# Moving float32 splits and a weight conversion between VectorE, GpSimd and two stages of a fused attention and two-MoE kernel

## The chip, the cores and the metric

The kernel runs on one core of one Trainium2 chip. The metric is the device time of one execution in microseconds (us). Of the core's engines these appear: TensorE (PE in the profile, with PEld for the loads of its weights), VectorE (DVE), ScalarE (ACT), GpSimd (POOL) and SyncE (SP), which issues most of the DMAs.

## What is computed

Three layers follow each other. An attention between `x` (4 batches, 8 heads, 512 positions, 64 lanes) and 32 state rows per batch gives 2176 tokens of 512 numbers. A dense mixture of 8 experts, whose weights P come from a softmax that is balanced eight times over rows and columns, follows, and then one wide gated layer:

```python
# first MoE
for e in range(E):                       # 8 experts, d_ff 1024
    h = np.maximum(x @ w1[e], 0.0)
    out += P[:, e:e + 1] * (h @ w2[e])
# second MoE: w_in 512x2048 and w_out 2048x512 are float64
h = x @ w_in
g = h * (1.0 / (1.0 + np.exp(-h)))
return g @ w_out
```

Products are made to float32 accuracy from three passes. Each operand is split into a high part (`fp32r`, a rounding) and a low part (the operand less its high part), and low times high, high times low and high times high are added up. So every operand costs a cast on ScalarE and a subtraction on another engine. The subtractions are what the change moves.

## The kernel before

The experts are cut into 16 units `u` of 512 hidden columns (two per expert), each with four 128x512 blocks of `w1` and four of `w2`. The work goes through five stages, of which four matter.

**Start and units 0 and 1 (0 to 250 us).** Attention, the first products, and units 0 and 1 for all four batches.

**Units 2 to 15 for batches 0 and 1 (some 252 to 840 us).** One unit takes some 47 us and has eight steps `k`: two batches times four blocks `f`. Step by step the loop at lines 1125 to 1263 issues: `S1` two steps ahead (the hidden block `ph`, its cast `hh` on ScalarE at L705, its low part `hl` on VectorE at L706), then `S2` (12 matmuls into four banks `po`). After the fourth block the four banks are weighted and added into `acc` by four VectorE instructions at L745. The pool `ps2` has four banks, so the next batch's first `S2`, and the state rows' product at k = 3, wait for these additions. At a unit's end k goes from 7 to 0 of the next unit. Weights are loaded ahead (`load_w1`, `load_w2`): the cast of a block is L243 on ScalarE, its low part is `lo_of` at L96, on the engine that `load_split` is given. In the kernel before this is VectorE for unit 1's `w1` and for `w2` of units 0 and 1, and GpSimd for all others. GpSimd also makes sums of `w2` blocks and their low parts (L213, L220) and the low parts of `G` (L668 through L96).

**The conversion.** `w_in` and `w_out` arrive as float64. A generator, `convert_all`, turns them into float32 high and low parts by integer operations on VectorE (L302 to L307: six instructions on 128x512 for one block, then L330 and L334, or L319 and L320, and for each pair of blocks the sums at L351 to L360) and stores them to DRAM. It has 40 items, ten for each quarter `v` of the hidden columns, and yields twice per item. In the kernel before `convert_some` draws it forward at 86 places: eight in unit 1 and six in each of units 2 to 14, with a pace of 0.99 yields per place, and `convert_some` puts each instruction behind the last `hl` on VectorE and the last `hh` on ScalarE.

**Batches 2 and 3 (some 840 to 1320 us).** A seven-product scheme (`block`, `product_b`) for the same units. The change doesn't touch it.

**Second MoE (some 1320 us to the end).** 16 phases `q`, of which the first eight are for the first half of the tokens; the phases 0 and 1 use the converted quarter v = 0, 2 and 3 use v = 1, and 6 and 7 use v = 3. A phase has seven products of six matmuls in the order 1, 5, 2, 6, 3, 7, 4 with the four parts of `second` (12 matmuls each, of the phase before) between them. `silu` makes a gated block: a sigmoid (L819), a product on VectorE (L820), a cast `gh` on ScalarE (L823) and the low part `gl` on VectorE (L824 through L96). The four banks of `ps2` hold the results `pr`, which VectorE adds into `res` (L851). In the first eight phases the state rows' product `s_second` comes right after the last part of `second` and takes a bank of the same pool.

TensorE's order is written out by hand. On the other engines a planner orders the instructions by the place where they are written and by its own estimate of when each becomes ready; the order is fixed before the kernel runs.

Of the kernel before, what the change touches and what calls it, by code (L numbers as in the profile page):

```python
# [21 lines left out]
def fused_kernel(ctx: ExitStack, tc: tile.TileContext, x, state, w_gate, w1, w2, w_in, w_out, out):  # L22
# [240 lines left out]
    def load_w1(u, hp, only_raw=False):  # L263
        e, fh = divmod(u, UPE)
        src = w1[e, hp * 128:(hp + 1) * 128, fh * FU:(fh + 1) * FU]
        if only_raw:
            load_raw(src, [128, FU], f"w1_{u}_{hp}")
        else:
            w1t[u, hp] = load_split(src, [128, FU], f"w1_{u}_{hp}", "w1", 4, nc.vector if u == 1 else nc.gpsimd)

    def load_w2(u, f, only_raw=False):
        e, fh = divmod(u, UPE)
        r0 = fh * FU + f * 128
        if only_raw:
            load_raw(w2[e, r0:r0 + 128, :], [128, DM], f"w2_{u}_{f}")
        else:
            w2t[u, f] = load_split(w2[e, r0:r0 + 128, :], [128, DM], f"w2_{u}_{f}", "w2", 5, nc.vector if u < UPE else nc.gpsimd)

# [102 lines left out]

    def ask_next(n):
        for one in items[n + 1:n + 3]:
            if one[0] is not item_sums:
                ask(one[1])
                return

    def convert_all():

        before = None  # L390
        for n in range(len(items) + 1):
            now, ops = None, []
            if n < len(items):
                make, *args = items[n]
                now = make(*args)
                ops = next(now)
            half = (len(ops) + 1) // 2
            if before:
                next(before)
            for op in ops[:half]:  # L400
                op()
            opens = n < len(items) and (items[n][0] is item_in and items[n][-1] == 0 or n and items[n - 1][0] is item_sums)
            if not opens:
                ask_next(n)
            yield
            for op in ops[half:]:
                op()
            if before:
                stored.append(next(before))
            if opens:  # L410
                ask_next(n)
            yield
            before = now
# [365 lines left out]
    def product(q, p):  # L779
# [23 lines left out]
        elif p == 5:  # L803
            kept("s5", "att", att)
        elif p == 2:
# [3 lines left out]
        elif p == 3:  # L809
            silu(q, 0, 1, summed("c12", ps, parts["u2"]))  # L810
        elif p == 7:
            kept("u3", "att", att)
            silu(q, 1, 1, summed("c22", parts["u3"], parts["s5"]))
        else:
            silu(q, 1, 0, ps)

    def silu(q, f, c, src):
        sg = att.tile([128, 512], F32, tag="e2", name=f"sg{q}_{f}_{c}", bufs=3)
        nc.scalar.activation(out=sg, in_=src, func=AF.Sigmoid)  # L819
        nc.vector.tensor_tensor(out=sg, in0=src, in1=sg, op=ALU.mult)  # L820
        hh = hp_.tile([128, 512], F32R, tag="hh", name=f"gh{q}_{f}_{c}")
        hl = hp_.tile([128, 512], F32R, tag="hl", name=f"gl{q}_{f}_{c}")
        nc.scalar.copy(hh, sg)  # L823
        lo_of(hl, sg, hh)  # L824
        blocks[q, f, c] = hh, hl
# [258 lines left out]

    convert_ops = convert_all()
    pace = 1.04 * 2 * (len(items) + 1) / (8 + (NU - UPE - 1) * 6)
    done = [0, 0]

    def convert_some():
        with tc.issue_after(last["dve"].ins), behind_rows():  # L1090
# [237 lines left out]
    s_load(0, 1)  # L1328

    for q, (g, v, fp) in enumerate(phases):  # L1330
        more = q + 1 < len(phases)
        earlier = [lambda: None] * 4 if q == 0 else [lambda n=n: second(q - 1, n) for n in range(4)]

        def step(p):
            product(q, p)
            if more:
                load_win(*phases[q + 1][1:], p)
            if q == 7 and p != 4:
                later = {1: 6, 5: 3, 2: 7, 6: 4}.get(p)
# [81 lines left out]
```

## Time and profile before

| | us |
|---|---|
| median of 3 runs | 1684.21 |
| lowest and highest | 1681.69, 1689.62 |
| the profiled execution | 1687.53 |
| its span, first to last instruction | 1685.5 |

| engine | busy us | share of the span | instructions |
|---|---|---|---|
| PE | 1628.7 | 97% | 7269 |
| DVE | 1148.2 | 68% | 1616 |
| ACT | 724.7 | 43% | 1231 |
| POOL | 717.9 | 43% | 455 |

The 97% is an average over stages. In some of them TensorE never stops, and in others it stops for a few microseconds per unit and then runs for a while at the lower clock. So the stages are to be read one by one: how long each engine is busy in it, which clock was granted, what ended TensorE's waits, and what the engine that it waited for did before. An idle GpSimd or ScalarE alone says nothing, and a busy VectorE costs something only where an instruction that TensorE needs stands behind others in its queue.

### The profile page before, as it was taken

The page shows a single profiled execution, that of the slowest core. Times are in us where ns is not written, and L with a number is a line of the kernel's source. Part 1 is how long each engine was busy: PE and PEld are TensorE (multiplying, and loading weights), DVE is VectorE, ACT ScalarE, POOL GpSimd, SP SyncE. Part 2 cuts the span into 40 slices and gives each one's busy share as a digit, 9 for nine tenths or more (in the row PEclk, how much of TensorE's full clock was granted, in tenths as well). Part 3 has the DMA queues.
Part 4 walks back from the last instruction along what each step waited for, and adds up shares of the span by engine and source line. Part 5 has one row for each costly group of instructions (what it writes and reads, how often), then busy time and mean ns, then how long its engine had stood idle before and what let it go on. Part 6 is the DMA issues. An engine that isn't in the chain of part 4 may idle for free.

```text
span 1685.5 us, 20967 instructions
## 1 busy us (share of the span) xinstructions
PE 1628.7 (97%) x7269; PEld 1302.0 (77%) x7269; DVE 1148.2 (68%) x1616; ACT 724.7 (43%) x1231; POOL 717.9 (43%) x455
## 2 busy tenths in 40 slices
PE   7999999899998999989999999999999999999999
PEld 5788777677776777767888888888888788888887
DVE  8924785776777767667636777767767656585565
ACT  5644346344443443434334444444544533343332
POOL 2011256666565655566546767666753400000000
PEclk9999999999999999999999999999999999999999
DMA  7042359757765776766436664544541654445442
GB/s 181 26 141 85 132 180 317 252 203 239 248 227 189 256 256 216 251 215 215 151 107 175 171 172 148 172 148 157 158 144 51 230 174 152 156 150 169 138 142 71
DMA packets 196394, 293.49 MB, mean 174 GB/s; under 512 B 35584, under 2 KB 82240, under 8 KB 196288
## 3 DMA queue, kind: packets, MB, share of 16 engines
q1 hardware_dynamic: 169552, 242.71, 46.0%
q10 hardware_dynamic: 26736, 49.44, 8.0%
q8 instruction: 58, 0.95, 0.2%
q14 instruction: 48, 0.39, 0.1%
HBM read 194.27 MB, written 97.81 MB: 173 GB/s over the span
## 4 chain that ended last, share of the span: by engine, by line
PE 78%; DVE 11%; DMA 3%; issue 3%; ACT 2%; POOL 2%; SPq 0%; ACTq 0%; DVEq 0%; POOLq 0%
PE pBa L980 8%; PE po L91 7%; PE po L92 6%; PE po L93 6%; PE pa L790 5%; PE pBc L980 4%; PE pr L92 3%; PE pr L93 3%; PE pr L91 3%; PE ph L91 3%; PE pB L93 3%; PE pB L91 3%; PE pB L92 3%; PE ph L93 3%; PE ph L92 3%; PE pc L790 3%
## 5 line engine op out<-in xcount | busy, mean ns | idle before, releaser
L91 PE MATMUL po<-h_w,hl 128*128 128x512 f32 x576 | 236.2, 410 | 22.2 <-DVE acc L745 20.7
L92 PE MATMUL po<-l_w,hh 128*128 128x512 f32 x576 | 231.2, 401 | 0.0
L93 PE MATMUL po<-h_w,hh 128*128 128x512 f32 x576 | 230.8, 401 | 0.0
L706 DVE SCALAR_TENSOR_TENSOR hl<-ph,hh 128x512 fp32r<-128x512 f32 x144 | 98.8, 686 | 184.8 <-ACT hh L705 184.6
L705 ACT ACTIVATE hh<-ph 128x512 fp32r<-128x512 f32 x144 | 86.2, 599 | 292.9 <-PE ph L93 289.7
L96 POOL TENSOR_TENSOR l_w<-raw,h_w 128x512 fp32r<-128x512 f32 x104 | 151.0, 1465 | 125.1 <-ACT h_w L243 112.7
L91 PEld LDWEIGHTS po<-h_w,hl 128*128 128x128 f32 x576 | 111.0, 193 | 62.4 <-DVE acc L745 25.7
L96 POOL TENSOR_TENSOR T<-t,T 128x512 fp32r<-128x512 f32 x84 | 113.3, 1349 | 82.1 <-ACT T L943 81.0
L980 PE MATMUL pBa<-T,wh 128*128 128x512 f32 x448 | 139.5, 392 | 0.5 <-DVE T L96 0.5
L93 PEld LDWEIGHTS po<-h_w,hh 128*128 128x128 f32 x576 | 111.4, 193 | 25.2
L92 PEld LDWEIGHTS po<-l_w,hh 128*128 128x128 f32 x576 | 111.6, 194 | 23.3 <-issue 0.2
L91 PE MATMUL ph<-aTh,G 128*128 128x512 f32 x288 | 118.4, 411 | 6.0 <-ACT stg L630 3.1
L943 ACT CAST T<-t 128x512 fp32r<-128x512 f32 x112 | 69.5, 621 | 115.6 <-DVE t L948 101.1
L220 POOL TENSOR_TENSOR w2s<-w2s,w2h 128x512 fp32r<-128x512 f32 x56 | 79.6, 1421 | 89.8 <-ACT w2h L219 86.9
L93 PE MATMUL ph<-aTh,G 128*128 128x512 f32 x288 | 114.0, 396 | 0.0
L92 PE MATMUL ph<-aTl,G 128*128 128x512 f32 x288 | 113.8, 395 | 0.0
L745 DVE SCALAR_TENSOR_TENSOR acc<-po,P,acc 128x512 f32<-128x512 f32 x112 | 77.6, 741 | 39.6 <-PE po L93 39.6
L96 POOL TENSOR_TENSOR G<-gf,G 128x1024 fp32r<-128x1024 f32 x32 | 77.6, 2424 | 60.9 <-ACT G L667 60.9
L93 PE MATMUL pr<-woh,gh 128*128 128x512 f32 x256 | 100.2, 391 | 0.0
L92 PE MATMUL pr<-wol,gh 128*128 128x512 f32 x256 | 100.1, 391 | 0.0
L91 PE MATMUL pr<-woh,gl 128*128 128x512 f32 x256 | 99.9, 390 | 0.0
L980 PEld LDWEIGHTS pBa<-T,wh 128*128 128x128 f32 x448 | 84.1, 188 | 19.8 <-DVE T L96 1.2
(268 smaller groups left out, 3916.9 us busy)
## 6 DMA issues: line engine op xcount, KB each, us to landing
g_d<-stg ACTq DMA_DIRECT2D x60, 512.0 KB, 4.3
wi<-wi_d SPq DMA_DIRECT2D x108, 256.0 KB, 3.0
raw<-in_moe_w_dram SPq DMA_DIRECT2D x104, 256.0 KB, 4.6
gf<-g_d SPq DMA_DIRECT2D x128, 128.0 KB, 4.1
w_d<-w2h ACTq DMA_DIRECT2D x56, 256.0 KB, 2.8
w_d<-w2s SPq DMA_DIRECT2D x56, 256.0 KB, 2.3
gfs<-g_d SPq DMA_DIRECT2D x112, 128.0 KB, 4.1
wh<-w_d SPq DMA_DIRECT2D x56, 256.0 KB, 3.4
```

The costliest lines, as they stand in the source:

```text
L91: nc.tensor.matmul(ps, al, bh, start=first, stop=False)
L92: nc.tensor.matmul(ps, ah, bl, start=False, stop=False)
L93: nc.tensor.matmul(ps, ah, bh, start=False, stop=last)
L96: engine.tensor_tensor(out=lo, in0=src, in1=hi.bitcast(F32), op=ALU.subtract)
L220: nc.gpsimd.tensor_tensor(out=t.bitcast(F32R), in0=t, in1=hi.bitcast(F32), op=ALU.subtract)
L705: last["act"] = nc.scalar.activation(out=hh, in_=ph, func=AF.Relu)
L706: last["dve"] = nc.vector.scalar_tensor_tensor(out=hl, in0=ph, scalar=0.0, in1=hh.bitcast(F32), op0=ALU.max, op1=ALU.subtract)
L745: nc.vector.scalar_tensor_tensor(out=a, in0=ps, scalar=P[:, t, e:e + 1], in1=a, op0=ALU.mult, op1=ALU.add)
L790: nc.tensor.matmul(ps, a, b, start=begin, stop=kp == 1 and i == 2, skip_group_check=True)
L943: nc.scalar.copy(hi, t)
L980: nc.tensor.matmul(ps, a, b, start=p in (1, 2, 5) and q == 0 and i == 0, stop=q == 1 and i == 2, skip_group_check=True)
```

## The change

Three things are moved. First, every low part of `w1` and `w2` of the first MoE is made by VectorE (the default of `load_split`). Second, the conversion's items 30 to 39 (the quarter v = 3) leave the first MoE. The pace there falls from 0.99 to 0.75 yields per place, and the ten items are drawn in the second MoE, at a pace of 0.62 yields per product from the product 7 of phase 0 to phase 5. `convert_some` now stands behind the gated product on VectorE (L820) and the cast `gh` on ScalarE, since `silu` sets `last`. Third, the low part `gl` is made by GpSimd. Two kept tiles (`s5`, `u3`) go from the pool `att` to the pool `raw`, since the conversion needs the slots of `att`.

```diff
-            w1t[u, hp] = load_split(src, [128, FU], f"w1_{u}_{hp}", "w1", 4, nc.vector if u == 1 else nc.gpsimd)
+            w1t[u, hp] = load_split(src, [128, FU], f"w1_{u}_{hp}", "w1", 4)
...
-            w2t[u, f] = load_split(w2[e, r0:r0 + 128, :], [128, DM], f"w2_{u}_{f}", "w2", 5, nc.vector if u < UPE else nc.gpsimd)
+            w2t[u, f] = load_split(w2[e, r0:r0 + 128, :], [128, DM], f"w2_{u}_{f}", "w2", 5)
...
-    def convert_all():
+    def convert_all(start, end):
...
         elif p == 5:
-            kept("s5", "att", att)
+            kept("s5", "raw", rawp)
...
         elif p == 7:
-            kept("u3", "att", att)
+            kept("u3", "raw", rawp)
             silu(q, 1, 1, summed("c22", parts["u3"], parts["s5"]))
...
         nc.scalar.activation(out=sg, in_=src, func=AF.Sigmoid)
-        nc.vector.tensor_tensor(out=sg, in0=src, in1=sg, op=ALU.mult)
+        last["dve"] = nc.vector.tensor_tensor(out=sg, in0=src, in1=sg, op=ALU.mult)
...
-        nc.scalar.copy(hh, sg)
-        lo_of(hl, sg, hh)
+        last["act"] = nc.scalar.copy(hh, sg)
+        lo_of(hl, sg, hh, nc.gpsimd)
...
-    convert_ops = convert_all()
-    pace = 1.04 * 2 * (len(items) + 1) / (8 + (NU - UPE - 1) * 6)
+
+    FIRST = len(items) // NV * (NV - 1)
+    convert_ops = convert_all(0, FIRST)
+    pace = 1.04 * 2 * (FIRST + 1) / (8 + (NU - UPE - 1) * 6)
     done = [0, 0]
 
-    def convert_some():
+    def convert_some(pace=pace):
...
+    ask(items[FIRST][1])
+    convert_ops = convert_all(FIRST, len(items))
+    done = [0, 0]
     for q, (g, v, fp) in enumerate(phases):
...
             product(q, p)
             if more:
                 load_win(*phases[q + 1][1:], p)
+            if 0 < q < 6 or q == 0 and p in (7, 4):
+                store()
+                convert_some(0.62)
```

## Rows read from the trace of the kernel before

**Rows 1.** Stretches in us: each engine's busy time (instructions), granted clock, DMA share.

```profile
252.00:840.00 588.00, 554.48 (x2434) 432.56 (x2433) 414.61 (x490) 255.39 (x444) 350.63 (x228) 0.97 0.69 232
...
1344.00:1470.00 126.00, 126.00 (x554) 102.67 (x553) 72.78 (x112) 40.32 (x68) 0.00 (x0) 1.00 0.48 157
...
0.00:84.00 84.00, 72.10 (x337) 54.37 (x338) 72.92 (x144) 51.02 (x95) 10.40 (x21) 0.96 0.40 104
```

**Rows 2.** TensorE's waits in 252 to 840 us: total, times, longest.

```profile
PE po L91 <- DVE acc L745: 20.7, 8, 4.7
PE pg L626 <- DVE hl L706: 8.5, 5, 2.6
```

**Rows 3.** Timeline of one unit's end (start us, us): VectorE, GpSimd, TensorE.

```profile
626.47 1.51 DVE L306 TENSOR_SCALAR cv<-cv 128x512 uint32<-128x512 uint32 x1
627.91 1.78 DVE L320 TENSOR_TENSOR cvo<-cv 128x512 fp32r<-128x512 f32 x1
629.61 1.78 DVE L307 SCALAR_TENSOR_TENSOR cv<-raw,cv 128x512 f32<-128x512 uint32 x1
...
631.92 0.68 DVE L706 SCALAR_TENSOR_TENSOR hl<-ph,hh 128x512 fp32r<-128x512 f32 x1
...
627.66 6.09 POOL L96 TENSOR_TENSOR l_w<-raw,h_w 128x512 fp32r<-128x512 f32 x4
...
633.31 0.50 PE L91 MATMUL po<-h_w,hl 128*128 128x512 f32 x1 [2.20 <-DVE acc L745]
```

**Rows 4.** Two units' ends as stretches, and the wait within the second.

```profile
633.00:638.00 5.00, 4.69 (x14) 3.72 (x15) 4.93 (x8) 0.00 (x0) 5.00 (x4) 0.66 0.34 105
726.00:733.00 7.00, 5.67 (x24) 4.36 (x24) 6.97 (x9) 1.95 (x4) 7.00 (x6) 1.00 0.64 196
...
727.33 0.50 PE L91 MATMUL po<-h_w,hl 128*128 128x512 f32 x1 [1.63 <-DVE acc L745]
```

**Rows 5.** Timeline of VectorE, 450 to 458 us: conversion instructions one by one.

```profile
450.87 1.21 DVE L360 TENSOR_TENSOR ws<-ws,wsh 128x1024 fp32r<-128x1024 f32 x1
452.01 0.41 DVE L306 TENSOR_SCALAR cv<-cv 128x512 uint32<-128x512 uint32 x1
452.45 0.69 DVE L307 SCALAR_TENSOR_TENSOR cv<-raw,cv 128x512 f32<-128x512 uint32 x1
...
456.06 1.39 DVE L304 TENSOR_SCALAR cv<-cv 128x512 uint32<-128x512 uint32 x1
```

**Rows 6.** VectorE's 15 conversion groups in 252 to 840 us: busy us, mean ns.

```profile
L304 DVE TENSOR_SCALAR cv<-cv 128x512 uint32<-128x512 uint32 x29 | 38.3, 1321 | 1.0
...
L351 DVE TENSOR_TENSOR ws<-wb 128x256 f32<-128x256 f32 x7 | 3.3, 478 | 0.0
```

**Rows 7.** Low parts (L96) by engine: ns min/median/max, first and last start.

```profile
L96 POOL TENSOR_TENSOR l_w<-raw,h_w x104: 1266/1464/2114, 227.9 to 855.2; 128x512 fp32r<-128x512 f32 x104
L96 POOL TENSOR_TENSOR l_w<-raw_w,h_w x16: 1267/1289/1491, 11.7 to 226.6; 128x512 fp32r<-128x512 f32 x16
...
L96 DVE TENSOR_TENSOR l_w<-raw_w,h_w x16: 651/685/693, 33.1 to 155.7; 128x512 fp32r<-128x512 f32 x16
...
L96 DVE TENSOR_TENSOR wl<-w2p,wh x42: 681/1016/2577, 853.8 to 1291.0; 128x512 fp32r<-128x512 f32 x42
...
L96 DVE TENSOR_TENSOR gl<-sg,gh x64: 681/692/694, 1334.6 to 1671.4; 128x512 fp32r<-128x512 f32 x64
```

**Rows 8.** Timeline at the end of phase 3 of the second MoE.

```profile
1404.35 0.69 DVE L820 TENSOR_TENSOR sg<-pa,sg 128x512 f32<-128x512 f32 x1 [0.64 <-ACT sg L819]
...
1404.96 1.88 DVE L851 TENSOR_TENSOR res<-pr,res 128x512 f32<-128x512 f32 x3
...
1406.20 0.40 PE L91 MATMUL prs<-woh,gls 128*128 128x512 f32 x1
```

**Rows 9.** Two stretches of the second MoE, columns as in the first group.

```profile
1386.00:1409.00 23.00, 23.00 (x104) 18.73 (x103) 13.70 (x21) 7.77 (x13) 0.00 (x0) 1.00 0.42 133
...
1470.00:1512.00 42.00, 42.00 (x184) 33.60 (x183) 35.46 (x48) 21.51 (x33) 0.00 (x0) 1.00 0.45 152
```

More of the change, by code (lines that the diff above doesn't have):

```diff
@@ L380, in fused_kernel, with ask_next @@
             sources.append(w_out[r0:r0 + 128])
-    def ask_next(n):
-        for one in items[n + 1:n + 3]:
+    def ask_next(n, end):
+        for one in items[n + 1:min(n + 3, end)]:
             if one[0] is not item_sums:
@@ L386, in ask_next @@
                 return
-    def convert_all():
+    def convert_all(start, end):
         before = None
-        for n in range(len(items) + 1):
+        for n in range(start, end + 1):
             now, ops = None, []
-            if n < len(items):
+            if n < end:
                 make, *args = items[n]
@@ L401, in convert_all @@
                 op()
-            opens = n < len(items) and (items[n][0] is item_in and items[n][-1] == 0 or n and items[n - 1][0] is item_sums)
+            opens = n < end and (items[n][0] is item_in and items[n][-1] == 0 or n and items[n - 1][0] is item_sums)
             if not opens:
-                ask_next(n)
+                ask_next(n, end)
             yield
@@ L410, in convert_all @@
             if opens:
-                ask_next(n)
+                ask_next(n, end)
             yield
```

## The prediction

> **What bounds the kernel now.** I read the stages first: TensorE's busy time and granted clock by stretch. In the second MoE it is busy 126.00 of 126 us at clock 1.00, so nothing can be won there, only lost. In the units 2 to 15 (252 to 840 us) it is busy 554.5 of 588 us, and the clock is 0.97 on average [rows 1]. The stage loses 588 - 554.5 = 33.5 us in stops and about 0.03 x 588 = 18 us by the clock; the second number overlaps the first a little. That is what a change in this stage can win, some 48 us, 2.9% of the kernel.
>
> Next the waits of that stage. 20.7 us in 8 waits are for `acc`, the additions that free the four result banks; 8.5 us are for `hl` [rows 2]. Both are VectorE's. Then the timeline of one such stop. VectorE works through conversion instructions of 1.51, 1.78 and 1.78 us while GpSimd makes four low parts in 6.09 us without a pause; then come `hl` and only then `acc`, and TensorE stands 2.20 us [rows 3]. The same instructions take 0.41 to 0.69 us elsewhere, and a one-operand one takes 1.39 us where GpSimd runs [rows 5]. So VectorE is late because each of its instructions waits for one of GpSimd's. After this stop the granted clock is 0.66 over 5 us, a part of it at 1.2 instead of 2.4 GHz; after a stop of 1.63 us it stays at 1.00 [rows 4].
>
> **The change part by part.** The profiled execution took 1687.5 us, its span 1685.5; the median of the runs is 1684.2. I make the sum against the profiled one and move the difference to the median.
>
> *Low parts to VectorE.* 104 + 16 instructions leave GpSimd, where they take 1464 and 1289 ns at the median. On VectorE the same shape takes 685 ns while GpSimd rests, and beside a busy GpSimd (`wl`, in the stage after) 1016 ns at the median, 2577 at most [rows 7]. So the price of one lies between 0.65 and 2.6 us; I take 0.685 and count the conflicts separately.
>
> *A quarter of the conversion leaves the stage.* Its 15 groups, from 38.3 down to 3.3 us, add up to 280 us in 252 to 840 [rows 6]. Bare, with 0.42 us for 114 one-operand instructions and 28 short ones, 0.69 for 117 others and 1.21 for seven long ones [rows 5], it would be 60 + 81 + 8 = 149 us. So conflicts cost 280 - 149 = 131 us, 0.57 us for each of GpSimd's 228 instructions there [rows 1].
>
> *VectorE's load in the stage.* Bare it was 414.6 - 131 = 284 us. It loses 37 (a quarter of 149) and gains 66 (96 of the 104 low parts, by 0.685): 313. GpSimd keeps 132 of 228 instructions; at 0.57 us these cost 75. Sum 388 us against 414.6, 6% less. With the low parts at `wl`'s median instead, 96 x 0.33 = 32 us more, it is 420, no relief. I take 388, since the conflicts are already in the 75.
>
> *What TensorE gets of it.* The average matters less than the unit's end. In the stop shown the three conversion instructions would cost 0.41 + 0.69 + 0.69 = 1.8 us instead of 5.1. The four low parts that ran beside them now stand in VectorE's own queue: 4 x 0.685 = 2.7. That is 4.5 instead of 5.1, and with a quarter of the conversion gone 4.0: 1.1 us earlier for each such end. It is not the whole stop, and there is a floor: `hl` is written before `acc` in VectorE's order [rows 3], and it needs the matmuls just before the stop; a stop of this kind still took 1.63 us where VectorE was least behind [rows 4]. With 8 waits averaging 2.6 us, 1.1 us off each is 9 us of 20.7. Bounds: 0, if the planner puts the low parts ahead of `acc`, and 20.7, if `acc` gets ahead of `hl`. Of the 8.5 us for `hl` I take 2 back, since the sums of `w2`, which run beside them on GpSimd, stay. Stops that shrink from 2.2 to near 1.6 us also stop halving the clock; a half-speed stretch like the one in [rows 4] loses 0.34 x 5 = 1.7 us, and I count four of them, 7 us. Together -18 us, bounds 0 and -44.
>
> *Unit 0 and the start.* Four low parts of unit 0 now lie on VectorE, which is busy 72.9 of the first 84 us [rows 1]: +2.7 us if all lie on the path, slightly below 0 since 685 ns follow the cast sooner than 1289 [rows 7]. I take +1. The other 20 before 252 us fall where VectorE has room.
>
> *The quarter in the second MoE.* Eight blocks by 4 x 0.42 + 4 x 0.69 = 4.4 us and two sums by 4 x 0.42 + 1.21 = 2.9 us are 41 us of VectorE, in 22 halves of 1.9 us. A pace of 0.62 gives 4.34 halves per phase, 8.1 us. The phase from 1386 to 1409 us has 13.7 us on VectorE [rows 9]; less four `gl` by 0.69 [rows 7] and with 8.1 it is 19.0 of 23 us, 83%. A stretch with 35.5 of 42 us, 84%, has no stop of TensorE [rows 9], so the load alone is no bound. The place is: `s_second` takes a result bank right after the last part of `second`. Today the gated product starts at 1404.35, the first addition at 1404.96, ending some 0.63 us later, and `prs` begins at 1406.20: 0.6 us to spare [rows 8]. A half of the conversion is written before these additions and tied behind that gated product. Where it goes first, the addition comes 1.9 us later and TensorE waits 1.3 us. Product 4 of the phases 1 to 4 is the 9th, 16th, 23rd and 30th place, and 0.62 times the place passes a whole number at the 9th, 23rd and 30th: 3 x 1.3 = 4 us. Bounds: 0, where the first addition slips in before, and 5 phases by a half of four instructions in conflict (4 x 1.5 - 0.6 = 5.4 us), 27 us. I take +4.
>
> *`gl` on GpSimd.* 64 low parts of some 1.29 us (the quiet row of [rows 7]) for 0.69. Each waits for `gh` as before and is read one phase later: hidden by several parts of `second`. At the very end the last one lies behind 24 matmuls: 0. If that cover went, 0.6 us each. *DMAs and queues.* The moved items bring 8 reads and some 28 stores on SyncE's queue, past the loads of the next phase's weights, which wait a phase ahead; DMA share is 0.48 [rows 1]: 0, with a store that waits for a late VectorE able to hold up a load by as much. The casts of the conversion queue behind `gh` on ScalarE, busy 7.8 of 23 us [rows 9]: 0.
>
> Sum: -18 + 1 + 4 = -13 us. 1687.5 - 13 = 1674.5 for the profiled execution, 1684.2 - 13 = 1671 us for the median.
>
> **The rivals.** *The order is the floor (same).* The low parts are written before `acc` and the planner lets them go first. VectorE then ends no earlier, the stops stay at 1.6 to 2.6 us, and only some clock comes back: -8 + 1 + 4 = -3, 1681 us. For it: `acc` stands behind `hl` in the rows now [rows 3]. Against it: the 131 us of conflicts do fall.
>
> *VectorE is never late (faster by more).* If the additions get ahead of `hl`, the 20.7 and most of the 8.5 us go, with 15 us of clock: -38 + 1 + 1 = -36, 1648 us. For it: every instruction in the stop is one in conflict. Against it: VectorE's load falls by 6% only.
>
> *The second MoE pays (slower).* GpSimd, idle there now (0.00 us), gets four instructions a phase, and VectorE's conversion and products with two operands in SBUF run into them as at 626 us [rows 1, 3]. The conversion's halves before `s_second` then cost 4 us more than the spare 0.6 in five phases, 20 us with a little clock, and the first MoE gives back only 8: +13, 1697 us. It decides from the point where the first addition starts over 0.6 us late. For it: the tight bank. Against it: 84% of VectorE carried no stop, without GpSimd though. The Trainium skill speaks for this rival: "GPSIMD Engine Reference", section "Key points", has GpSimd share its SBUF interfaces with VectorE and contend with two-port modes and two-input instructions, and calls VectorE about twice as fast for elementwise work; by that rule `gl` should not go to GpSimd, and the sum would be this rival's 1697 us. Of the first MoE the rows agree with it (1.39 for 0.41 us).
>
> *The relief doesn't come (slower).* The low parts take `wl`'s 1.0 us and more beside the remaining sums; VectorE is busy for 420 us, the stops stay and the units' ends get 0.5 us longer: +5 + 1 + 4 = +10, 1694 us.
>
> **How the numbers follow.** Forecast 0.45, floor 0.23, never late 0.13, the second MoE pays 0.13, no relief 0.06. A measurement tells 0.5%, 8.4 us, from no change. The forecast spans -21 to -5 us, and four fifths of it lie below -8.4. Faster: 0.36 + 0.02 + 0.13 + 0 = 0.51; slower: 0.12 + 0.05 = 0.17; same: 0.32. The range goes from 1648, the end of the large gain, to 1693, most of the slower cases left in.
>
> **What would show it.** In the profile after: the stage's stops and its 0.97; conversion instructions in 252 to 840 us with means nearer to 0.7 than to 1.2 us; `l_w` on VectorE at 0.7 to 1.0 us; VectorE near 390 us there; waits of `po` for `acc` in fewer or shorter pieces; in the second MoE waits of `prs` for `res` of 1 to 2 us at the ends of phases 1, 3 and 4. The prediction is wrong if `acc` waits are as long as before with short conversion instructions (then the order is the floor), or if TensorE falls below 122 of 126 us in the second MoE.

## The result and the profile after

| | before | after |
|---|---|---|
| median, us (4 runs each, side by side) | 1686.49 | 1657.62 |
| lowest to highest, us | 1681.69 to 1689.62 | 1656.88 to 1657.85 |
| the profiled execution, us | 1687.53 | 1656.88 |
| its span, us | 1685.5 | 1654.9 |

The ratio is 0.9831 with an interval of 0.9803 to 0.9858: 28.9 us, 1.7% faster. The forecast was 13 us; the sign and the range held, the size was less than half of the gain. The profiled execution of the kernel before lies 3.3 us above the median that the forecast started from, so the two profiles are 30.6 us apart and the medians 28.9.

To see where the time went, the span is cut at marks that TensorE passes in both kernels: the first product with the state rows of the first MoE, the first matmul for the batches 2 and 3, the first of the second MoE, and the end (differences from unrounded marks).

| part of the span, us | before | after | difference | forecast |
|---|---|---|---|---|
| start | 137.3 | 138.5 | +1.2 | +1 |
| first MoE, batches 0 and 1 | 750.8 | 707.8 | -43.0 | -18 |
| batches 2 and 3 | 436.0 | 437.6 | +1.7 | 0 |
| second MoE | 361.4 | 371.0 | +9.6 | +4 |

So two terms were too small, with opposite signs. First the page of the kernel after, its busy times:

```profile
PE 1613.4 (97%) x7269; PEld 1291.0 (78%) x7269; DVE 1115.6 (67%) x1672; ACT 724.5 (44%) x1231; POOL 635.5 (38%) x399
```

TensorE has the same 7269 instructions and is busy for 15.3 us less: the same matmuls ran at a higher granted clock. The share is 97% as before and shows nothing. The stages do. These are stretches of the kernel after, columns as in [rows 1] (length, busy us of PE, PEld, DVE, ACT, POOL with instructions, granted clock, DMA share, GB/s):

```profile
252.00:798.00 546.00, 536.50 (x2422) 420.27 (x2421) 361.08 (x517) 249.72 (x435) 211.04 (x131) 0.99 0.69 227
...
287.00:763.40 476.40, 471.68 (x2140) 369.00 (x2140) 320.44 (x465) 216.35 (x377) 182.24 (x113) 1.00 0.70 230
...
1306.00:1432.00 126.00, 118.73 (x515) 95.30 (x514) 103.98 (x159) 46.20 (x79) 31.21 (x20) 1.00 0.74 240
```

The first line answers to the first of [rows 1]. The second goes from the state rows' product of one unit to that of unit 15; it holds the same some 2140 matmuls in every kernel here. In the kernel before it is:

```profile
285.10:804.80 519.70, 487.65 (x2141) 379.32 (x2140) 371.06 (x436) 220.24 (x385) 311.03 (x201) 0.97 0.69 232
```

The stretch is 519.70 - 476.40 = 43.3 us shorter, all of the stage's gain. 487.65 - 471.68 = 16.0 us of it is clock (the same matmuls take less), and the stops fell from 519.70 - 487.65 = 32.1 us to 476.40 - 471.68 = 4.7. The last of the three stretches of after stands against the second of [rows 1]: TensorE had no gap in 126 us of the second MoE and now has 7.3 us of them.

TensorE's waits in the kernel after, 252 to 798 us (total, times, longest), against [rows 2]:

```profile
PE pg L626 <- DVE hl L706: 7.0, 4, 4.8
PE po L91 <- DVE acc L745: 2.3, 2, 1.7
```

The 20.7 us for `acc` are 2.3. Of the waits for `hl` 4.8 us are a single stop at 269 us. Now the timeline of one unit's end after, which answers to [rows 3] (start, duration, engine, line, instruction, in brackets the idle time before it and what ended it):

```profile
596.41 1.78 DVE L320 TENSOR_TENSOR cvo<-cv 128x512 fp32r<-128x512 f32 x1
...
598.72 1.28 DVE L96 TENSOR_TENSOR l_w<-raw,h_w 128x512 fp32r<-128x512 f32 x2
...
600.52 1.88 DVE L96 TENSOR_TENSOR l_w<-raw,h_w 128x512 fp32r<-128x512 f32 x3
602.33 0.68 DVE L96 TENSOR_TENSOR hsl<-pt,hsh 128x512 fp32r<-128x512 f32 x1
602.97 0.69 DVE L706 SCALAR_TENSOR_TENSOR hl<-ph,hh 128x512 fp32r<-128x512 f32 x1
603.58 2.72 DVE L745 SCALAR_TENSOR_TENSOR acc<-po,P,acc 128x512 f32<-128x512 f32 x4
...
604.47 2.42 POOL L96 TENSOR_TENSOR G<-gf,G 128x1024 fp32r<-128x1024 f32 x1 [6.83 <-ACT G L667]
...
602.34 0.60 ACT L705 ACTIVATE hh<-ph 128x512 fp32r<-128x512 f32 x1 [0.81 <-PE ph L93]
...
606.04 0.40 PE L93 MATMUL ph<-aTh,G 128*128 128x512 f32 x1
606.27 0.39 PE L91 MATMUL po<-h_w,hl 128*128 128x512 f32 x1
```

GpSimd idles for 6.83 us, five low parts take 3.16 us on VectorE, and the four additions stand where they stood, behind `hsl` and `hl`. TensorE goes from `ph` to `po` without a gap. One instruction (L320, 1.78 us) still ran beside one of GpSimd's, the low part of a sum (L220), which ran from 595.86 us on.

VectorE's groups in the same stretch (count, busy us, mean ns, idle us before), against [rows 6] and the first of [rows 7]:

```profile
L96 DVE TENSOR_TENSOR l_w<-raw,h_w 128x512 fp32r<-128x512 f32 x96 | 77.6, 838 | 0.0
...
L304 DVE TENSOR_SCALAR cv<-cv 128x512 uint32<-128x512 uint32 x21 | 18.1, 860 | 0.5
```

The mean of L304 fell from 1321 to 860 ns, and a low part costs 838 ns: its bare 685 and some 150 of hold-up.

TensorE's waits of the kernel after from 1284 us to the end:

```profile
PE prs L91 <- DVE res L849: 3.2, 1, 3.2
PE prs L91 <- DVE res L851: 3.0, 3, 1.5
PE pa L790 <- ACT u L794: 1.2, 1, 1.2
PE psf L91 <- DMA wr<-wr_d: 1.1, 1, 1.1
PE pst L1021 <- DVE c L798: 0.5, 1, 0.5
```

6.2 us of the 9.0 are waits of `prs` for the additions, as the forecast had named them. The longest in the timeline, which answers to [rows 8]:

```profile
1320.54 1.27 POOL L96 TENSOR_TENSOR gl<-sg,gh 128x512 fp32r<-128x512 f32 x1 [0.51 <-ACT gh L823]
1320.57 1.79 DVE L334 TENSOR_TENSOR cvi<-wb,cvi 128x512 fp32r<-128x512 f32 x1
...
1322.28 2.47 DVE L849 COPY res<-pr 128x512 f32<-128x512 f32 x4
...
1323.01 0.50 PE L91 MATMUL prs<-woh,gls 128*128 128x512 f32 x1 [3.20 <-DVE res L849]
```

A conversion instruction that takes 0.68 us alone begins 0.03 us after GpSimd's `gl`, takes 1.79, and the first copy out of the four banks starts behind it.

### The profile page after: what moved, and what is told of

Read it like the earlier page. It is cut to its first block, busy times and chain, and to the rows that moved or that the text cites. A ratio compares the mean times of both kernels' runs of the same rounds, so it can differ in the third digit from the quotient of the medians.

```text
span 1654.9 us, 21019 instructions
## 1 busy us (share of the span) xinstructions
PE 1613.4 (97%) x7269; PEld 1291.0 (78%) x7269; DVE 1115.6 (67%) x1672; ACT 724.5 (44%) x1231; POOL 635.5 (38%) x399
## 4 chain that ended last, share of the span: by engine, by line
PE 79%; DVE 13%; DMA 3%; ACT 2%; issue 2%; SPq 0%; POOL 0%; DVEq 0%; ACTq 0%; POOLq 0%
PE pBa L980 9%; PE po L91 7%; PE po L92 7%; PE po L93 7%; PE pBc L980 4%; PE pa L790 4%; PE ph L91 3%; PE ph L93 3%; PE ph L92 3%; PE pB L93 3%; PE pB L91 3%; PE pB L92 3%; PE pr L92 3%; PE pr L93 3%; PE pr L91 3%; PE pg L626 2%
## 5 line engine op out<-in xcount | busy, mean ns | idle before, releaser
L706 DVE SCALAR_TENSOR_TENSOR hl<-ph,hh 128x512 fp32r<-128x512 f32 x144 | 98.9, 687 | 202.4 <-ACT hh L705 202.0
L91 PE MATMUL po<-h_w,hl 128*128 128x512 f32 x576 | 230.2, 400 | 2.3 <-DVE acc L745 2.3
L93 PE MATMUL po<-h_w,hh 128*128 128x512 f32 x576 | 226.2, 393 | 0.0
L92 PE MATMUL po<-l_w,hh 128*128 128x512 f32 x576 | 226.0, 392 | 0.0
L96 POOL TENSOR_TENSOR gl<-sg,gh 128x512 fp32r<-128x512 f32 x64 | 88.2, 1382 | 260.9 <-ACT gh L823 254.1
L96 POOL TENSOR_TENSOR G<-gf,G 128x1024 fp32r<-128x1024 f32 x32 | 78.7, 2458 | 273.3 <-ACT G L667 257.6
L96 POOL TENSOR_TENSOR T<-t,T 128x512 fp32r<-128x512 f32 x84 | 113.2, 1348 | 82.0 <-ACT T L943 81.9
L220 POOL TENSOR_TENSOR w2s<-w2s,w2h 128x512 fp32r<-128x512 f32 x56 | 79.7, 1423 | 147.7 <-ACT w2h L219 137.3
L790 PE MATMUL pa<-x,wi 128*128 128x512 f32 x372 | 96.8, 395 | 1.2 <-ACT u L794 1.2
```

Source lines behind the costliest of these rows:

```text
L91: nc.tensor.matmul(ps, al, bh, start=first, stop=False)
L92: nc.tensor.matmul(ps, ah, bl, start=False, stop=False)
L93: nc.tensor.matmul(ps, ah, bh, start=False, stop=last)
L96: engine.tensor_tensor(out=lo, in0=src, in1=hi.bitcast(F32), op=ALU.subtract)
L220: nc.gpsimd.tensor_tensor(out=t.bitcast(F32R), in0=t, in1=hi.bitcast(F32), op=ALU.subtract)
L706: last["dve"] = nc.vector.scalar_tensor_tensor(out=hl, in0=ph, scalar=0.0, in1=hh.bitcast(F32), op0=ALU.max, op1=ALU.subtract)
```

## The experiments

Times are medians beside runs of the kernel before on the same chip (1682.7 to 1685.6 us); the interval of each ratio is in brackets. Over the chips the kernel before differs by 3.8 us (1682.7 to 1686.5), so a few microseconds between two changed kernels that ran on different chips prove nothing; such cases are read from the profiles. Two words: an instruction of VectorE meets one of GpSimd's when it runs beside it, and what it then takes over its bare time is its hold-up. The theory: VectorE's instructions are held up by GpSimd's, one part of the change takes these meetings away, another brings some into the second MoE. The rivals: what counts is VectorE's load, so that the quarter of the conversion that leaves the first MoE makes the gain; or it is where the instructions stand in its order.

### One part at a time

**Low parts alone**, against the kernel before:

```diff
-            w1t[u, hp] = load_split(src, [128, FU], f"w1_{u}_{hp}", "w1", 4, nc.vector if u == 1 else nc.gpsimd)
+            w1t[u, hp] = load_split(src, [128, FU], f"w1_{u}_{hp}", "w1", 4)
...
-            w2t[u, f] = load_split(w2[e, r0:r0 + 128, :], [128, DM], f"w2_{u}_{f}", "w2", 5, nc.vector if u < UPE else nc.gpsimd)
+            w2t[u, f] = load_split(w2[e, r0:r0 + 128, :], [128, DM], f"w2_{u}_{f}", "w2", 5)
```

> The kernel before with one part of the change: VectorE makes all low parts of w1 and w2, the whole conversion stays in the first MoE. Theory (VectorE is late at a unit's end because GpSimd's low parts hold it up instruction by instruction): most of the 42 us that the change won by the first product of batches 2 and 3 (888.1 to 846.3 us) comes from this part alone, so some 25 to 35 us less than before, waits of po for acc under 6 us in all (20.7 before), and the second MoE as long as before (361 us). Rival (the amount of VectorE's work decides): bare work rises by 66 us with nothing taken away, so the time is the same as before or up to 10 us longer, and the acc waits stay at 20 us or more.

Measured: 1640.29 us, ratio 0.9734 [0.9715, 0.9754]: 44 us faster than before, more than the theory's 25 to 35, and 17 us faster than the whole change. TensorE's waits in 252 to 795 us:

```profile
PE po L91 <- DVE acc L745: 2.8, 2, 2.3
PE pg L626 <- DVE hl L706: 0.2, 1, 0.2
```

The mark of batches 2 and 3 comes 46.8 us earlier than before, and the second MoE takes 361.5 us, as before. So the low parts make all of the gain, and the rest of the change costs 17 us.

**The quarter alone**, against the kernel after: the two lines above back as they were, and

```diff
-        lo_of(hl, sg, hh, nc.gpsimd)
+        lo_of(hl, sg, hh)
```

> The changed kernel with the low parts of w1 and w2 back on GpSimd as before, and the low part of the gated rows back on VectorE: only the quarter of the conversion is moved. Theory (conflicts): the conversion at a unit's end still runs into GpSimd's low parts, only a quarter less of it: 5 to 15 us won in the first MoE, waits of po for acc still 10 us or more; the second MoE 3 to 9 us longer, since the draws ahead of the state rows' product stay; sum between -10 and +3 us. Rival (load): VectorE loses some 70 us of busy time in the stage, more than in the whole change, so the stage wins as much as there, 35 to 42 us, and the kernel is 25 us or more faster than before.

Measured: 1690.11 us, ratio 1.0042 [1.0026, 1.0058]. TensorE's waits in 252 to 838 us:

```profile
PE pg L626 <- DVE hl L706: 16.0, 7, 4.1
PE po L91 <- DVE acc L745: 11.3, 5, 3.7
PE ph L91 <- ACT stg L630: 2.5, 1, 2.5
```

In the profile the mark of batches 2 and 3 comes 2.3 us earlier (theory: 5 to 15), and the second MoE is 4.3 us longer. What `acc` waits less, `hl` waits more. The median is 5.7 us above that of before, outside the theory's -10 to +3, and the load rival's 25 us are far off; that the quarter alone wins anything in the first MoE isn't shown.

**`gl` alone**, against the kernel before:

```diff
-        lo_of(hl, sg, hh)
+        lo_of(hl, sg, hh, nc.gpsimd)
```

> The kernel before with one part of the change: GpSimd makes the low part of the gated rows in the second MoE. Theory: VectorE has no conversion there to be held up, and the additions from a result bank with one operand in SBUF are not held up (0.69 us at most everywhere); only gated products with both operands in SBUF are. TensorE never waited there, so no difference: within 3 us of before. Rival (the contention by itself costs TensorE time in the second MoE): 10 us or more longer, with waits of prs or pr for res.

Measured: 1684.29 us, ratio 0.9993 [0.9979, 1.0007]. No difference in the medians; in the profile the second MoE is 0.8 us longer, and `prs` waits 0.6 us for `res`. Without the conversion beside it, `gl` on GpSimd is nearly hidden.

### Load or meetings

Here the stretch of 2140 matmuls is read in each kernel, columns as above.

**The low parts made again by GpSimd**, over the same tile, against the kernel after, where `twin` is `u != 1` for `w1` and `u >= UPE` for `w2`:

```diff
         lo_of(lo, raw, hi, engine)
+        if twin:
+            lo_of(lo, raw, hi, nc.gpsimd)
```

> The changed kernel, where GpSimd makes each low part of w1 and w2 that was taken from it once more, over the same tile after VectorE has made it (the same values). VectorE's own work and the conversion are those of the changed kernel; only GpSimd's 120 instructions are back. Theory (conflicts): conversion and low parts on VectorE take 1.2 to 1.8 us again at the units' ends, the acc waits come back (15 us or more), and 20 to 45 us of the change's 42 us in the first MoE are lost. Rival (load or place of VectorE's work): GpSimd's extra work is off the path, within 5 us of the changed kernel, acc waits under 5 us.

Measured: 1744.15 us, ratio 1.0358 [1.0335, 1.0381], 86.5 us over the kernel after and nearly twice what I had set as the most. The matmuls that read the tile must wait for the repeats as well, so the time of this run can hold more than the price of the meetings; but from 301 to 848 us all of TensorE's listed waits are for VectorE (30.6 us for `hl`, 17.8 for `acc`), none for GpSimd. VectorE's low parts there:

```profile
L96 DVE TENSOR_TENSOR l_w<-raw,h_w 128x512 fp32r<-128x512 f32 x88 | 104.3, 1214 | 0.4
```

Each costs 1214 ns in place of 838, with the same VectorE instructions. And the stretch:

```profile
301.10:847.90 546.80, 498.24 (x2140) 385.55 (x2139) 388.98 (x465) 216.54 (x377) 313.63 (x201) 0.95 0.61 200
```

VectorE's 465 instructions are those of the kernel after. They are busy for 388.98 us in place of 320.44: 68.5 us of hold-up from 88 more instructions of GpSimd, 0.78 us for each.

**The low parts made twice by VectorE**, against the kernel with the low parts alone, where `twin` is `u > 1` for `w1` alone:

```diff
         lo_of(lo, raw, hi, engine)
+        if twin:
+            lo_of(lo, raw, hi, engine)
```

> The kernel with all low parts of w1 and w2 on VectorE, in which VectorE makes the low part of every w1 block of the units 2 to 15 twice, into the same tile. It tells VectorE's load apart from its meetings with GpSimd. Some 45 repeats by 0.685 us bring VectorE in the stretch of units 4 to 15 from 345 to about 376 us, as much as in the kernel with w2's low parts alone moved (377 us, 1693.0 us) and more than in the kernel before (371 us); GpSimd's 113 instructions stay as they are. Theory A, the load: VectorE ends a unit as late as in that kernel, waits of po for acc add up to 15 to 40 us and the time is 1670 to 1700 us. Theory B, the meetings: a load without more GpSimd instructions is not late at the units' ends; the acc and hl waits stay under 6 us and the time is 1639 to 1650 us.

Measured: 1668.62 us, ratio 0.9894 [0.9872, 0.9916], 1.4 us under theory A's range and 19 us over theory B's. TensorE's waits in 252 to 820 us (the lines stand two further down in this kernel):

```profile
PE po L91 <- DVE acc L747: 21.3, 10, 5.8
PE pg L628 <- DVE hl L708: 2.2, 1, 2.2
```

and the stretch:

```profile
287.50:786.80 499.30, 477.87 (x2139) 371.43 (x2139) 373.30 (x568) 220.05 (x385) 192.82 (x113) 0.98 0.72 242
```

GpSimd's 113 instructions are the same and VectorE's load is 29 us up: the time rises by 28 us, and the waits for `acc` are back. So load counts too, and the theory that named the meetings alone fell.

The same stretch with the low parts alone:

```profile
283.90:758.40 474.50, 471.64 (x2140) 369.71 (x2139) 344.62 (x525) 219.97 (x385) 182.52 (x113) 1.00 0.76 254
```

and with the quarter alone:

```profile
292.10:802.40 510.30, 484.58 (x2141) 376.87 (x2140) 326.22 (x380) 216.30 (x377) 303.10 (x200) 0.98 0.65 215
```

These two say the opposite of load: VectorE has 18 us less to do with the quarter alone, and the stretch is 36 us longer; GpSimd has 200 instructions there and not 113. Neither sum alone orders the kernels.

### Half of the low parts

Against the kernel before, those of `w2`:

```diff
-            w2t[u, f] = load_split(w2[e, r0:r0 + 128, :], [128, DM], f"w2_{u}_{f}", "w2", 5, nc.vector if u < UPE else nc.gpsimd)
+            w2t[u, f] = load_split(w2[e, r0:r0 + 128, :], [128, DM], f"w2_{u}_{f}", "w2", 5)
```

and in a second kernel those of `w1`:

```diff
-            w1t[u, hp] = load_split(src, [128, FU], f"w1_{u}_{hp}", "w1", 4, nc.vector if u == 1 else nc.gpsimd)
+            w1t[u, hp] = load_split(src, [128, FU], f"w1_{u}_{hp}", "w1", 4)
```

> The kernel before, where VectorE makes the low parts of w2 alone (56 instructions leave GpSimd), those of w1 stay on GpSimd. Theory (each low part of GpSimd costs VectorE one hold-up): about half of the 44 us, 15 to 28 us faster than before. Rival (a threshold: VectorE catches up once a part of the hold-ups is gone): 35 us or more, or under 8 us.

> The kernel before, where VectorE makes the low parts of w1 alone (64 instructions leave GpSimd), those of w2 stay on GpSimd. Theory (each low part costs one hold-up): about half of the 44 us, 15 to 28 us faster than before. Rival (a threshold): 35 us or more, or under 8 us, and not the same as with w2 alone.

Measured: `w2` alone 1693.03 us, ratio 1.0045 [1.0026, 1.0065]; `w1` alone 1713.64 us, 1.0174 [1.0157, 1.0191]. Both were expected faster and are slower, while both together save 44 us: +8, +29, and -44. TensorE's waits for `acc` grew from 20.7 to 39.7 and 56.4 us. The stretch with `w2`'s low parts moved:

```profile
282.10:810.50 528.40, 488.56 (x2140) 380.40 (x2139) 377.22 (x481) 220.38 (x385) 250.77 (x157) 0.95 0.68 229
```

and with those of `w1`:

```profile
286.30:831.90 545.60, 489.06 (x2140) 380.09 (x2139) 395.80 (x480) 220.47 (x385) 251.90 (x157) 0.94 0.66 222
```

VectorE takes over 44 low parts, 30 us bare, and its load rises by 6 and by 25 us over the 371.06 before: by this sum the 44 instructions that leave GpSimd bring back 24 and 5 us of hold-up (0.54 and 0.12 each), less than the new work. With all 88 gone it falls by 26 us in spite of 60 us more work: 87 us back, 1.0 each. These prices are estimates from the loads. Why the second half brings so much more than the first is seen at a unit's end, here with `w1`'s moved (timeline, 691 to 704 us):

```profile
692.85 1.78 DVE L307 SCALAR_TENSOR_TENSOR cv<-raw,cv 128x512 f32<-128x512 uint32 x1
694.55 2.85 DVE L320 TENSOR_TENSOR cvo<-cv 128x512 fp32r<-128x512 f32 x1
697.32 1.75 DVE L330 TENSOR_TENSOR wb<-cv 128x512 f32<-128x512 f32 x1
...
700.79 0.68 DVE L706 SCALAR_TENSOR_TENSOR hl<-ph,hh 128x512 fp32r<-128x512 f32 x1
...
694.03 2.81 POOL L96 TENSOR_TENSOR G<-gf,G 128x1024 fp32r<-128x1024 f32 x1
696.81 1.71 POOL L213 TENSOR_TENSOR w2s<-raw,w2s 128x512 f32<-128x512 f32 x1
...
702.18 0.80 PE L91 MATMUL po<-h_w,hl 128*128 128x512 f32 x1 [6.58 <-DVE acc L745]
```

What GpSimd has left still runs almost without a pause at this unit's end until 698.52 us, so each conversion instruction shown meets one of its instructions, and VectorE's queue ahead of `acc` is longer by the low parts. In the kernel after GpSimd idles there for 6.83 us, and in the kernel with the low parts alone for 6.56 at one such end (ahead of its `G` at 557.51 us). That it is this pause which the second half opens was read from such ends, not tried by itself. It also stays open why `w2` alone, with the same load as the kernel with twins on VectorE (377 and 373 us), is 24 us slower: it has 44 more GpSimd instructions, but how much of the 24 is place and how much meetings isn't told apart.

### The place of the conversion

**No draws at a unit's end**, against the kernel before:

```diff
-        if more and k % NF != NF - 1:
+        if more and k in (0, 1, 2, 4):
...
-    pace = 1.04 * 2 * (len(items) + 1) / (8 + (NU - UPE - 1) * 6)
+    pace = 1.04 * 2 * (len(items) + 1) / (8 + (NU - UPE - 1) * 4)
```

> The kernel before, where the steps 5 and 6 of a unit no longer draw a half of the conversion and the four steps 0, 1, 2 and 4 draw one and a half each; GpSimd keeps all its low parts and the conversion stays whole in the first MoE. Theory (VectorE is late at the unit's end because conversion and GpSimd's four low parts in a row meet there): waits of po for acc fall from 20.7 to under 8 us, but the conversion meets the sums of w2 on GpSimd in steps 0 to 4, so waits of pg for hl rise above 8.5 us; in all 0 to 15 us faster than before. Rival (the place doesn't matter, VectorE is late throughout): acc waits stay at 15 us or more.

Measured: 1691.91 us, ratio 1.0050 [1.0032, 1.0067]. The waits for `acc` fall to 2.6 us in 252 to 842 us, those for `hl` rise to 24.9, both as the theory had it; the time doesn't: it is 9 us longer, where 0 to 15 us shorter were expected. The hold-up moves to another place of the unit; it doesn't go.

**`gl` back on VectorE**, against the kernel after:

```diff
-        lo_of(hl, sg, hh, nc.gpsimd)
+        lo_of(hl, sg, hh)
```

> The changed kernel with the low part of the gated rows back on VectorE (two parts of the change: the low parts of w1 and w2, and the quarter of the conversion). Theory A (place: the halves of the conversion stand ahead of the additions that free the bank for the state rows' product): GpSimd isn't needed for that loss, the second MoE stays 6 to 14 us longer than before, since VectorE now also keeps 2.8 us per phase, and prs still waits for res; 1655 to 1664 us. Theory B (conflict: the loss comes from GpSimd running into the conversion): the loss in the second MoE falls to 3 us or less, some 1648 to 1652 us.

Measured: 1652.59 us, ratio 0.9811 [0.9791, 0.9831], just above theory B's range. The median is 5 us under that of the kernel after, but the two ratios to the kernel before (0.9811 and 0.9831) have overlapping intervals, so the medians alone don't settle it. TensorE's waits from 1280 us on:

```profile
PE prs L91 <- DVE res L849: 1.2, 1, 1.2
PE psf L91 <- DMA wr<-wr_d: 0.8, 1, 0.8
PE pa L790 <- ACT u L794: 0.7, 1, 0.7
PE prs L91 <- DVE res L851: 0.6, 2, 0.4
```

In the profile the second MoE is 4.1 us longer than before, not 9.6. With the quarter alone it was 4.3. So in the profiles the quarter's place costs 4 us, more than theory B's 3 and less than theory A's 6, and `gl` on GpSimd beside it 5.5 us; `gl` without it costs 0.8.

**No draw behind product 4**, against the kernel after:

```diff
-            if 0 < q < 6 or q == 0 and p in (7, 4):
+            if 0 < q < 6 and p != 4 or q == 0 and p in (7, 4):
                 store()
-                convert_some(0.62)
+                convert_some(0.72)
```

> The changed kernel, where product 4 of the phases 1 to 5 no longer draws a half of the conversion and the other products draw at a pace of 0.72 instead of 0.62, so the same ten items are done. Theory (place): the waits of prs for res (6.2 us in four places) fall to 1 us or less, the kernel is 4 to 7 us faster than the changed one, 1651 to 1654 us. Rival (load: VectorE has too much in these phases wherever it is put): the waits move to other instructions, within 2 us of the changed kernel.

Measured: 1654.22 us, ratio 0.9823 [0.9804, 0.9843]; the median is 3.4 us under that of the kernel after, less than the 4 to 7 expected, and by the ratios no difference is shown. In the profile the waits of `prs` fall from 6.2 to 1.1 us and the second MoE is 5.8 us longer than before, not 9.6. So the draws behind product 4 are most of these stops, and of the second MoE's loss they are some 4 of 9.6 us. What is left of the waits are above all those for `wr` by DMA (2.2 us) and for `u` (1.2).

**Low parts and `gl`, and low parts but those of unit 0's `w1`**, each against the kernel with the low parts alone:

```diff
-        lo_of(hl, sg, hh)
+        lo_of(hl, sg, hh, nc.gpsimd)
```

```diff
-            w1t[u, hp] = load_split(src, [128, FU], f"w1_{u}_{hp}", "w1", 4)
+            w1t[u, hp] = load_split(src, [128, FU], f"w1_{u}_{hp}", "w1", 4, nc.gpsimd if u == 0 else nc.vector)
```

> The kernel before with two parts of the change: all low parts of w1 and w2 on VectorE and the gated rows' low part on GpSimd; the conversion stays whole in the first MoE. Theory: GpSimd's part in the second MoE costs nothing by itself, so 1638 to 1643 us, as with the low parts alone, and the quarter of the conversion is all that separates this from the changed kernel's 1657.6 us. Rival (the parts need each other: with VectorE's faster second MoE something else comes out): more than 4 us from 1640.3 us.

> The kernel before with the low parts of w1 and w2 on VectorE, but those of unit 0's w1 on GpSimd as before, and the conversion whole in the first MoE. Theory: the start (the first product of state rows at 139.7 us with all low parts on VectorE, 137.3 us before) gets its 2 us back, some 1638 us, 1 to 3 us less than the 1640.3 us with all of them on VectorE. Rival: the start is bound by something else, no difference (within 1 us in the profile at that mark).

Measured: 1642.23 us, ratio 0.9754 [0.9736, 0.9771], and 1640.11 us, 0.9740 [0.9726, 0.9755]. The first differs from the low parts alone by 1.9 us, and in its profile the second MoE is 1.6 us longer: the quarter is what separates these from the kernel after, in both stages. In the second the mark at the start comes at 137.7 us in place of 139.7, but the median is the same: of the 2 us at the start 1.4 are left at the end of the profiled executions (spans 1637.4 and 1638.8), which the medians don't tell.

The marks of all these profiled executions tell the parts apart better than the medians. From the first mark to that of batches 2 and 3 it is 750.8 us in the two kernels that leave the first MoE alone (before, `gl` alone), 749.1 with the quarter gone, 701.6 to 701.8 with the low parts moved and the conversion whole (three kernels), and 705.9 to 707.8 with both (three kernels). So beside the low parts the quarter's leaving doesn't help the first MoE but costs it 4 to 6 us. The second MoE takes 361.4 to 361.5 us in six kernels that leave it alone and 362.9 in a seventh, 362.2 and 363.1 with `gl` alone, 365.5 and 365.7 with the quarter alone, and 371.0 and 375.0 with both (the last in the kernel with GpSimd's repeats). The two together cost more than the sum of each.

## Why the prediction was right or wrong

**What bounds the kernel: right.** The gain lies in the units 2 to 15, in the stops and the clock, as [rows 1, 2] had it; and the meetings make VectorE late, as [rows 3, 5] had it: GpSimd's repeats alone made the same 465 VectorE instructions 68.5 us longer. They aren't the only way to lateness, since VectorE's own repeats, with GpSimd's instructions unchanged in number, cost 28 us of the gain. The stage offered some 48 us by the forecast; 43.0 came.

**The floor: wrong, the step that failed.** I had written that `hl`, ahead of `acc` in the order, "needs the matmuls just before the stop", so a stop couldn't fall under some 1.63 us. The order is indeed unchanged after. But that `hl` belongs to the hidden block one step earlier. In the timeline of the kernel before, around the stop of [rows 3]:

```profile
627.02 0.60 ACT L705 ACTIVATE hh<-ph 128x512 fp32r<-128x512 f32 x1 [0.81 <-PE ph L93]
...
630.72 0.39 PE L93 MATMUL ph<-aTh,G 128*128 128x512 f32 x1
```

The cast that it needs ended at 627.62 us, and `hl` began at 631.92 [rows 3], 4.3 us late. The matmuls up to the stop serve the next `hh`. So the whole stop was lateness, and it could go to nothing: after, the cast starts at 602.34 us and `hl` at 602.97. The end of 1.63 us in [rows 4] was lateness too, not a floor: there the cast ended at 722.21 us, and `hl` began 3.7 us later.

```profile
721.61 0.60 ACT L705 ACTIVATE hh<-ph 128x512 fp32r<-128x512 f32 x1 [0.81 <-PE ph L93]
...
725.94 0.67 DVE L706 SCALAR_TENSOR_TENSOR hl<-ph,hh 128x512 fp32r<-128x512 f32 x1
```

Whoever had looked for the `hh` of that `hl` on ScalarE would have seen it.

**The average load: mis-sized, and of less use than thought.** Forecast 388 us for VectorE in the stage, measured 361.1. If the bare work was the 313 us of the forecast, the hold-up was 361.1 - 313 = 48 us in place of 75, or 0.37 for each of GpSimd's 131 instructions and not 0.57: an estimate, as the 0.57 was. A fixed price per GpSimd instruction doesn't hold: the runs gave 0.12, 0.54, 0.78 and 1.0 us.

**What TensorE gets: -18 forecast, -43.0 measured, at the end of its bounds of 0 and -44.** In the stretch of the same matmuls the stops gave 27.3 us (forecast 9 + 2) and the clock 16.0 (forecast 7). Both follow from the floor: I let the stops shrink, and they vanished. Then hardly any half-speed piece is left, and the clock is 1.00 in place of 0.97. One long stop stays ahead of that stretch, 4.8 us up to 269.7 us, with a clock of 0.59 over the 5 us after it; the kernel with the low parts alone doesn't have it. There the conversion's L302 had waited 2.40 us for its read, L303 behind it took 2.55 us beside GpSimd's `G`, and `hl` stood behind them; why that read comes late is open.

**The quarter leaving: taken as a gain, none shown.** I had not given it a price of its own; in the sum it carried 0.5 of the 1.1 us per unit's end. Alone it makes the first MoE 1.7 us shorter in the profile while the median rises, and beside the low parts the stage is 4 to 6 us longer without it.

**The start: right within the spread**, +1.2 against +1. Over the runs the first mark comes at 136.3 to 137.7 us where GpSimd makes the low parts of unit 0's `w1` alone, and at 137.8 to 140.7 where VectorE alone does.

**The quarter in the second MoE: the size right alone, +4.1 and +4.3 against +4, in part by luck.** The place named is there: `prs` behind the additions, behind a half that was drawn after product 4. But these waits are only 1.8 of the 4.1 us; 0.8 are for `wr`, and the matmuls take 1.4 us longer. The phases were not quite those counted (in the kernel after the stops fell in 1, 2, 3 and 5, not 1, 3 and 4).

**`gl` on GpSimd: wrong beside the quarter.** I put 0, since its own result is hidden; alone that nearly holds (0.8 and 1.6 us in the profiles). What I left out of the sum, and named in a rival only, is that it makes the conversion's instructions longer: 1.79 us at 1320 us. This was 5.5 us in the profiles. So that rival's mechanism was there, at a price of 9.6 us for the stage where it had put 20, and against a first MoE that gave back 43 us, not 8. For this stage the prediction's own sign of being wrong came true: it had set 122 of 126 us, and TensorE was busy for 118.7.

**Queues and DMA: nearly.** Forecast 0; the waits for `wr` cost 1.1 us, in a stretch where the DMA share is 0.74 in place of 0.48. The 1.7 us in batches 2 and 3 stay unexplained; over all the runs, which share this stage, it takes 434.9 to 437.6 us.

**The sum.** The two large errors have opposite signs, -25 us in the first MoE and +5.6 in the second, so the total came nearer to the forecast than its main term did. That much is luck.

**The rivals.** "VectorE is never late" came nearest in the first MoE (-36 forecast in all, at 1648 us), though not by its condition: the additions didn't get ahead of `hl`, `hl` itself came in time. It had spoken against itself by the load falling "by 6% only"; what counted were the instructions just ahead of `acc`. "The order is the floor" and "the relief doesn't come" fell.

The Trainium skill, "GPSIMD Engine Reference", section "Key points", names contention of GpSimd with VectorE's two-port modes and with instructions of two SBUF inputs. The runs here agree for two inputs in SBUF, where 0.68 us became 1.78; instructions that read a bank of PSUM (L706, L745) never took over 0.693 and 0.752 us before or after. Instructions with one operand were held up too, 1.39 us [rows 5] in place of some 0.42; no run here shows whether they ran in a two-port mode. The same section has VectorE about twice as fast for elementwise work; here it is 685 to 1289 ns for a low part [rows 7]. As a reason against `gl` on GpSimd it held beside the conversion (5.5 us in the profiles) and hardly without it (ratio 0.9993).

## What to carry to other kernels

Where two engines hold each other up, look at what stands in the late engine's queue just ahead of the instruction that TensorE waits for, and find the moment at which that instruction's own input was ready: as far as that difference goes the stop can shrink (here 4.3 us of lateness for a stop of 2.20), with the clock on top. Moving work off the disturbing engine paid only when its share at that place was gone: each half of the move lost, the whole won 44 us. And run the parts of a bundled change alone: here the low parts by themselves take 1640.3 us, 17 us less than the whole, because the quarter that was moved along costs 9.6 us, with `gl`, in the stage it enters and gives nothing in the one it leaves.

## What the runs showed of the hardware that was not expected

- A VectorE instruction with both operands in SBUF that meets one of GpSimd's lasts longer, and longer beside a longer one: a 128x512 subtraction takes 0.68 us alone, 1.78 beside a low part or a sum of 128x512, and 2.85 beside GpSimd's 128x1024 `G` (2.81 us).
- The hold-up isn't proportional to GpSimd's instruction count: by the loads, 44 fewer gave back some 24 or 5 us, and 88 fewer some 87 us.
- A stage with 32 us of stops had lost another 16 us by the clock; when the stops went, so did the clock's part. With the low parts alone moved, TensorE was busy for 471.6 of 474.5 us at clock 1.00.
